# The first expert's first list closed with batch 3, its tokens turned inside attention's last iterations

## The chip, the cores and the metric

The kernel runs on one core of a Trainium2 chip. The metric is the time of one launch on the device in microseconds (us), as the median over runs; lower is better. The core has a matrix engine (PE, whose weight loads the profile shows as PEld), three engines for elementwise work (DVE, ACT, POOL) and a queue that only issues transfers (SP). Each engine works through its own instructions in order and waits on semaphores for the others. POOL also issues the indirect transfers, those whose rows are picked by a list of indices.

## The reference

Local and global attention, followed by a mixture of experts with a skip test. What matters here:

```
attention, for each of 8 batches and 8 heads, head_dim 64:
    512 local queries see the 32 global keys and local keys at distance <= 32
    32 global queries see all 544 keys
x = attention output as (8 * 544, 512) rows
do = x @ w_skip > 0                      # other rows leave unchanged
e  = argmax(x @ w_gate)                  # one of 8 experts
g  = softmax(x @ w_gate)[e]
out[do] = x + g * (relu(x @ w1[e]) @ w2[e])      # w1 512 x 1024, w2 1024 x 512
```

Rows belong to a batch; row r of batch b is row 544 b + r of the output. For the inputs that the reference draws, 1980 rows pass the skip test, and the experts get 395, 171, 153, 289, 173, 371, 253 and 175 of them. Expert 0 gets 243, 7, 31, 7, 15, 3, 84 and 5 from the eight batches in turn.

## The kernel before

**Attention** is a loop over u = 0 to 33 (`NU` = 32 pairs of heads, four pairs to a batch, and two iterations to drain). It is written out by hand as a software pipeline: in iteration u the scores and exponentials of pair u (`scores`, L344) run beside the scaling (POOL, `scale`, L396), the transposes (`turn`, L432) and the values (`values`, `values_g`, L470 and L495) of pairs u-1 and u-2. `turn(0)` is copied out of PSUM by DVE, `turn(1)` by ACT. `gather_g` (L511) reduces the global queries' part on DVE. The order of the instructions on PE, DVE, ACT and POOL is the order of the program text (`manual_schedule`).

**Rows and routing.** When the four pairs of a batch are done, `batch_rows` (L651) turns its output into rows, writes them to `out` through SP (L543, L551) and computes the logits. Batches 5 and 6 have theirs in iterations 25 to 29; those of batch 7 begin in iteration 31 and end behind the loop (L814, L815). `route` (L574) makes a list of some twenty small steps for two batches together, (0,1), (2,3), (4,5), or for one, 6 and 7. The steps wait in `stages`; each call of `seam()`, seven in an iteration, takes one or two of them through `tick`. The running count of each expert stands in `base`, from which each token gets its slot in the expert's list `lst` in DRAM. The last stage puts the batch's sends into the queue `sends`: one indirect transfer from POOL (L639) for every 128 rows, which writes row number and gate weight to the slots. `send_some(n)` issues n of them.

**The first list.** The first 256 slots (`GRP`) of an expert are its first group. After batch 6 the count of expert 0 is lifted to at least 256 (L700), so no row of batch 7 lands in its first group. At the end of iteration 31 all stages are worked off, all sends issued and the group's list is read by SP (`slots`, L106); in iteration 32 DVE turns the row numbers to integers (`index`, L102) and POOL gathers the 256 rows into `xfirst` (`gather`, L119), two transfers of 128 rows out of the first seven batches' part of `out`.

**The experts.** Behind the loop the attention pools are released and `turn_x` (L832) makes the transposed input of the first group: for each of two halves four transposes on PE, a cast to float32r on ACT (`xh`) and the rest on DVE (`xl`). `ffn` (L848) then does 8 steps of 12 matmuls (`ph`), each followed by relu on ACT (`hh`) and its rest on DVE (`hlw`), and for each half 8 steps of 3 matmuls (`py`); `hook(i)` inserts other work after step i. In the first expert: after step 1 the steps of batch 7's routing, its sends and the reading of all other lists; after steps 4 to 7 the split of the second expert's weights; after step 9 `rest`, with the index and gather of the second expert's first group; after step 22 its `turn_x`. Weights arrive as float32 tiles `raw` through SP and are split in two parts by ACT and DVE (L181, L184). A group beyond the first is done behind it, at full width if more than 128 rows remain, otherwise by `ffn_half`.

## Time and profile before

| what | before |
|---|---|
| median of three runs | 502.44 us (500.73 to 504.15) |
| the profiled execution | 503.73 us |
| its span, first to last instruction | 502.0 us |
| mean granted clock of PE | 0.986 |
| PE busy | 455.9 us, 91% |
| DVE, ACT, POOL busy | 298.7, 289.6, 228.2 us |
| moved by DMA | 93.32 MB, mean 186 GB/s |

A row of the timeline has the start in us from the span's start, the length, engine, line, operation, output and inputs, shapes and count; in brackets stands the idle time of that engine just before and what ended it. A row of a group has busy time and the mean ns of one behind the bar. A row of the windows has for each engine its busy us with the number of instructions, then the granted clock of PE, the busy share of the DMA engines and GB/s. Matmuls are pipelined, so their lengths overlap; the distance from start to start is their pace.

### The profile page before, as it was taken

Reading aid. Unit: us, or ns where it says so; the run is one execution under the profiler, and the core shown is the slowest. Engines: PE = TensorE matmul, PEld = TensorE weight load, DVE = VectorE, ACT = ScalarE, POOL = GpSimd, SP = SyncE. Lnnn points to the kernel's source line nnn. Section 1 sums busy time; section 2 is a strip of 40 time slices with the busy share of each in tenths; the row PEclk is TensorE's granted clock in tenths of the full one; section 3 lists DMA queues with packets and bytes.
Section 4 is the critical chain, followed back from the end, with each engine's and each line's share of the span. In section 5 each row is a group of like instructions: output and inputs, shape, how many; then the busy total and the mean of one; then the engine's idle time right before and its main releaser. Section 6 shows DMA issues by size and latency. Waiting matters only on the chain. (4 is left out here: it accounts for less than half of the span.)

```text
span 502.0 us, 13663 instructions
## 1 busy us (share of the span) xinstructions
PE 455.9 (91%) x4962; PEld 368.5 (73%) x4962; DVE 298.7 (59%) x1221; ACT 289.6 (58%) x883; POOL 228.2 (45%) x236
## 2 busy tenths in 40 slices
PE   8799999999989998887698999999989999899991
PEld 3576767776666767666696979898968888688881
DVE  6886767877757767784453229684714757047310
ACT  4689999899868887764341208563514545145210
POOL 6656666669864677776246014323202341013300
PEclk9999999999999999999899999999999999899996
DMA  8899898889957788610547308883820949113100
GB/s 252 267 329 262 268 288 279 254 281 219 289 171 244 226 189 255 169 45 2 172 146 216 109 26 268 313 295 121 286 99 10 343 142 327 38 23 131 46 15 17
DMA packets 50545, 93.32 MB, mean 186 GB/s; under 512 B 15596, under 2 KB 19948, under 8 KB 50448
## 3 DMA queue, kind: packets, MB, share of 16 engines
q1 hardware_dynamic: 44624, 81.83, 52.0%
q0 software_dynamic: 5824, 10.25, 6.2%
q8 instruction: 55, 0.90, 0.9%
q14 instruction: 42, 0.34, 0.3%
HBM read 82.91 MB, written 14.67 MB: 194 GB/s over the span
## 5 line engine op out<-in xcount | busy, mean ns | idle before, releaser
L368 ACT ACTIVATE prob<-prob,nmx 128x160 f32<-128x160 f32 x256 | 106.4, 418 | 17.9 <-DVE nmx L363 15.7
L398 POOL TENSOR_TENSOR prob<-prob,inv 128x640 f32<-128x640 f32 x64 | 80.3, 1257 | 61.1 <-DVE ing L428 24.0
L863 ACT ACTIVATE hh<-ph 128x256 fp32r<-128x256 f32 x72 | 27.7, 385 | 83.2 <-PE ph L858 71.8
L940 POOL DMA_INDIRECT out_dram<-yo,six x12 | 12.2, 1018 | 134.6 <-DVE yo L939 116.7
L874 PE MATMUL py<-w2h,hh 128*128 128x512 f32 x144 | 57.2, 397 | 0.0
L874 PE MATMUL py<-w2h,hlw 128*128 128x512 f32 x144 | 56.9, 395 | 0.0
L874 PE MATMUL py<-w2l,hh 128*128 128x512 f32 x144 | 56.7, 394 | 0.0
L351 PE MATMUL pss<-ks,qs 64*64 64x160 f32 x1024 | 51.5, 305 | 3.1 <-DVE nmx L363 1.6
L864 DVE SCALAR_TENSOR_TENSOR hlw<-ph,hh 128x256 fp32r<-128x256 f32 x72 | 30.3, 421 | 32.4 <-ACT hh L863 29.6
L351 PEld LDWEIGHTS pss<-ks,qs 64*64 64x64 f32 x1024 | 34.1, 134 | 20.9 <-issue 15.2
L858 PE MATMUL ph<-xh,w1h 128*128 128x256 f32 x288 | 46.4, 283 | 3.2 <-ACT xh L844 1.5
L482 PEld LDWEIGHTS pv<-ptT,vw 128*64 128x64 f32 x1024 | 39.4, 137 | 13.3 <-issue 3.9
L368 ACT ACTIVATION_READ_ACCUMULATOR prob<-prob,nmx 128x1 f32 x256 | 48.4, 189 | 0.0
L482 PE MATMUL pv<-ptT,vw 128*64 128x64 f32 (+1 forms) x1024 | 44.2, 237 | 3.4 <-ACT ptT L441 1.6
L858 PE MATMUL ph<-xh,w1l 128*128 128x256 f32 x288 | 45.5, 280 | 0.0
L858 PE MATMUL ph<-xl,w1h 128*128 128x256 f32 x288 | 45.4, 280 | 0.0
L858 PEld LDWEIGHTS ph<-xh,w1h 128*128 128x128 f32 x288 | 39.3, 191 | 5.9 <-issue 3.8
L639 POOL DMA_INDIRECT lst<-dat,slu x34 | 34.3, 1008 | 18.0 <-DVE cni L959 9.6
L858 PEld LDWEIGHTS ph<-xh,w1l 128*128 128x128 f32 x288 | 39.1, 190 | 0.0
L858 PEld LDWEIGHTS ph<-xl,w1h 128*128 128x128 f32 x288 | 39.0, 190 | 0.0
L438 PE MATMUL pst<-ident,prob 128*128 128x128 f32 x256 | 36.6, 281 | 2.5 <-POOL prob L398 1.2
L184 DVE TENSOR_TENSOR w1l<-raw,w1h 128x1024 fp32r<-128x1024 f32 x28 | 34.1, 1220 | 6.6 <-ACT w1h L181 4.1
(178 smaller groups left out, 942.3 us busy)
## 6 DMA issues: line engine op xcount, KB each, us to landing
raw<-in_w_dram SPq DMA_DIRECT2D x60, 512.0 KB
vw<-in_v_dram SPq DMA_DIRECT2D x32, 512.0 KB
ks<-in_kT_dram SPq DMA_DIRECT2D x32, 400.0 KB
out_dram<-xr SPq DMA_DIRECT2D x32, 256.0 KB
qs<-in_qT_dram SPq DMA_DIRECT2D x31, 256.0 KB
vgs<-in_vgl_dram SPq DMA_DIRECT2D x32, 64.0 KB
raw<-in_w_dram POOLq DMA_DIRECT2D x4, 512.0 KB
lst<-dat,slu POOLq DMA_INDIRECT x34
```

What stands on the lines that cost most here:

```text
L184: eng.tensor_sub(lo, raw, hi.bitcast(F32))
L351: nc.tensor.matmul(banks[odd][head(h ^ odd), j * W:(j + 1) * W], q[head(h), w * QB:(w + 1) * QB], window(k[head(h)], w), start=True, stop= ...
L368: nc.scalar.activation(pt[:, i, :], pt[:, i, :], AF.Exp, bias=nmx[:, i:i + 1], scale=-1.0, accum_out=sums[:, i, 0:1],)
L398: nc.gpsimd.tensor_mul(pt[:, sl, :], pt[:, sl, :], inv[:, sl].unsqueeze(2).to_broadcast([P, 4, W]),)
L438: nc.tensor.transpose(pst[:, i * P:(i + 1) * P], pt[:, 4 * hf + i, 0:KW], ident)
L482: nc.tensor.matmul(pv[head(h), j * 96:j * 96 + n], vv[:, w, head(h)], ptT[:, w, h ^ odd, 0:n], start=j == 0, stop=False, skip_group_check= ...
L639: ins = nc.gpsimd.indirect_dma_start(out=lst, out_offset=bass.IndirectOffsetOnAxis(ap=slu[:, t:t + 1], axis=0), in_=dat[:, bs[j], t - 4 * ...
L858: nc.tensor.matmul(ph[:, 0:GRP], hl[a][:, c, f * P:(f + 1) * P], bb[:, c, :], start=i == 0, stop=i == 3 * NC - 1,)
L863: nc.scalar.activation(hh[:, f, :], ph[:, 0:GRP], AF.Relu)
L864: nc.vector.scalar_tensor_tensor(hlw[:, f, :], ph[:, 0:GRP], 0.0, hh[:, f, :].bitcast(F32), ALU.max, ALU.subtract,)
L874: nc.tensor.matmul(py, a[:, f, ts_], hl[bb][:, f, :], start=f == 0 and i == 0, stop=f == NF - 1 and i == 2,)
L940: ins = nc.gpsimd.indirect_dma_start(out=out, out_offset=bass.IndirectOffsetOnAxis(ap=sidx, axis=0), in_=yo, in_offset=None, bounds_check= ...
```

## The change

The list of expert 0 is closed after the routing of batches 2 and 3 instead of after batch 6. It is read in iteration 29, its index and gather stand in iteration 30, and the gather reads only the first four batches' part of `out`. `turn_x` and the tiles of the first `xh` and `xl` move ahead of the loop, into the pool that lives throughout; iterations 32 and 33 turn one half of the tokens each, with the cast in two parts. The sends that are ready in iterations 29 to 31 are issued later: two in iteration 29, none in 30, two in 31, the others at the seams of iterations 32 and 33 (before: four at the end of 29, one at each seam of 30 and 31 and four at their ends, and all that were left at the end of 31). The memsets of `xsecond` and `xmore` move from the start of the experts into `rest`, ahead of the gathers there.

```diff
+    xs = [
+        [const.tile([P, NC, GRP], F32R, name=f"x{part}{i}") for part in "hl"] for i in range(1)
+    ]
+
+    def turn_x(xg, i, ts=range(NSUB)):
+        xh, xl = xs[i]
+        for t in ts:
+            pt = ps_t("xt")
+            for c in range(NC):
+                nc.tensor.transpose(
+                    pt[:, c * P:(c + 1) * P], xg[:, t, c * P:(c + 1) * P], ident
+                )
+            p3 = pt.rearrange("p (c n) -> p c n", n=P)
+            ts_ = slice(t * P, (t + 1) * P)
+            step = NC if len(ts) > 1 else NC // 2
+            for c in range(0, NC, step):
+                nc.scalar.copy(xh[:, c:c + step, ts_], p3[:, c:c + step])
+            nc.vector.tensor_sub(xl[:, :, ts_], p3, xh[:, :, ts_].bitcast(F32))
+        return xh, xl
...
-                if b == B - 2:
+                if b == B // 2 - 1:
                     stages.append(
                         lambda: nc.vector.tensor_scalar_max(base[:, 0:1], base[:, 0:1], float(GRP))
                     )
...
                 def seam():
                     tick(1 if u < NU - 4 else 2)
-                    if u >= NU - 2:
+                    if u >= NU:
                         send_some(1)
...
                     cur.scores(1)
+                if u == NU - 3:
+                    slots(first, 0)
+                if u == NU - 2:
+                    index(first, 0)
+                    gather(xfirst, six[:, 0, 0, :], B // 2 * S)
+                if u >= NU:
+                    turn_x(xfirst, 0, (u - NU,))
                 while subs:
                     subs.pop()()
...
-                if u == NU:
-                    index(first, 0)
-                    gather(xfirst, six[:, 0, 0, :], (B - 1) * S)
...
-                send_some(2 if u < NU - 3 else 4)
+                send_some(4 if u >= NU else 2 if u != NU - 2 else 0)
                 seam()
                 prev, old = cur, prev
                 if u == NU - 1:
                     tick(len(stages))
-                    send_some(len(sends))
-                    slots(first, 0)
...
-    for t in (xsecond, xmore):
-        nc.gpsimd.memset(t, 0.0)
...
+    xs.append([f1.tile([P, NC, GRP], F32R, name=f"x{part}1") for part in "hl"])
...
-        x2 = turn_x(xfirst, 0)
+        x2 = xs[0]
         tick(13)
...
         def rest():
+            for t in (xsecond, xmore):
+                nc.gpsimd.memset(t, 0.0)
             index(slice(1, E), 0)
             index(slice(0, E), 1)
             gather(xsecond, six[:, 1, 0, :])
```

## What was expected

> **What bounds the kernel now.** I read the page's head first, then the timeline of TensorE (PE) around the end of attention, then the granted clock in short windows, then the queues of DVE, ACT, POOL and SP at that place.
>
> ```profile
> span 502.0 us, 13663 instructions
> PE 455.9 (91%) x4962; PEld 368.5 (73%) x4962; DVE 298.7 (59%) x1221; ACT 289.6 (58%) x883; POOL 228.2 (45%) x236
> ```
>
> PE is busy 91% of the span, so the time falls only where PE's idle or slow stretches fall. The timeline of PE has one such stretch where the first expert begins (start, length, line, count, idle before it and what ended it):
>
> ```profile
> 239.95 0.63 PE L531 MATMUL pr<-idw,xTg 128*128 128x137 f32 x4
> 241.66 0.63 PE L837 MATMUL xt<-ident,xfirst 128*128 128x128 f32 x4 [1.08 <-DMA xfirst<-out_dram,six]
> 244.42 0.63 PE L837 MATMUL xt<-ident,xfirst 128*128 128x128 f32 x4 [2.13 <-DMA xfirst<-out_dram,six]
> 245.73 1.22 PE L858 MATMUL ph<-xh,w1h 128*128 128x256 f32 x4 [0.68 <-ACT xh L844]
> 250.24 0.72 PE L858 MATMUL ph<-xh,w1h 128*128 128x256 f32 x4
> 253.15 0.63 PE L858 MATMUL ph<-xh,w1h 128*128 128x256 f32 x4
> 254.56 0.63 PE L858 MATMUL ph<-xh,w1h 128*128 128x256 f32 x4
> 269.06 0.40 PE L874 MATMUL py<-w2h,hlw 128*128 128x512 f32 x1
> 270.81 1.29 PE L837 MATMUL xt<-ident,xsecond 128*128 128x128 f32 x8 [1.35 <-DMA xsecond<-out_dram,six]
> ```
>
> Attention's last matmul ends at 240.58 and the expert's first starts at 245.73: 5.15 us, of which 3.89 are idle (1.08, 2.13, 0.68) and 1.26 turn the tokens. What ends the waits is the gather of xfirst. A second wait, 1.35 us before 270.81, is for the gather of xsecond. Then the clock (window, PE busy, ..., PEclk, DMA share, GB/s):
>
> ```profile
> 241.90:245.30 3.40, 1.02 (x8) 0.57 (x6) 0.69 (x1) 0.80 (x2) 0.64 (x1) 1.00 0.79 275
> 245.30:248.70 3.40, 2.97 (x14) 2.97 (x15) 2.73 (x13) 0.62 (x3) 0.00 (x0) 0.50 0.34 79
> 269.20:272.60 3.40, 2.02 (x13) 1.30 (x11) 0.51 (x1) 1.05 (x2) 3.10 (x5) 1.00 0.70 229
> 429.60:433.00 3.40, 1.80 (x9) 1.28 (x9) 0.68 (x1) 0.65 (x2) 0.00 (x0) 1.00 0.03 10
> 433.00:436.50 3.50, 3.50 (x10) 2.69 (x10) 0.01 (x1) 0.00 (x0) 0.00 (x0) 0.51 0.02 5
> ```
>
> After a window with PE busy 1.02 us of 3.4 the clock is 0.50 for the next 3.4; 1.80 us busy lets it fall too, 2.02 us does not. So the gap costs twice: the expert's groups of 12 matmuls come every 1.41 us later on (253.15 to 254.56), but the first two take 245.73 to 250.24 = 4.51, where 2 x 1.41 and some 0.28 for the counts between them make 3.10. Loss: 1.41 us.
>
> **The change part by part.** *The turn leaves the seam.* Gather, eight transposes, casts and subtractions are no longer between 240.58 and 245.73: -5.15 us, and with the gap the slow clock behind it: -1.41 us.
>
> *It comes back in iterations 32 and 33,* half the tokens in each, ahead of work that these end on:
>
> ```profile
> 233.55 0.65 ACT L509 COPY xT<-pv 128x256 f32<-128x256 f32 x2 [2.27 <-PE pv L501]
> 233.95 0.29 DVE L516 TENSOR_REDUCE xTg<-pv 128x32 f32<-128x128 f32 x1 [2.40 <-ACT xT L509]
> 233.64 1.10 PE L438 MATMUL pst<-ident,prob 128*128 128x128 f32 x8
> 234.68 0.65 DVE L441 COPY ptT<-pst 128x512 f32<-128x512 f32 x1
> 235.43 0.80 PE L482 MATMUL pv<-ptT,vw 128*64 128x96 f32 x14 [0.69 <-ACT ptT L441]
> 237.50 0.65 ACT L509 COPY xT<-pv 128x256 f32<-128x256 f32 x2 [2.13 <-PE pv L501]
> 238.74 1.78 ACT L536 COPY xr<-pr 128x256 f32<-128x256 f32 x4 [0.59 <-PE pr L531]
> L845 DVE TENSOR_TENSOR xl<-xt,xh 128x512 fp32r<-128x512 f32 x20 | 13.1, 687 | 25.4 <-ACT xh L844 25.4
> L844 ACT CAST xh<-xt 128x256 fp32r<-128x256 f32 x4 | 1.3, 375 | 11.7 <-PE xt L837 11.7
> ```
>
> In iteration 32 PE turns after the values at 233.6 (0.63, beside idle time). ACT casts twice (375 ns each, a half per cast) after its two xT copies, until about 234.85. DVE's subtraction (687 ns) waits for that and stands ahead of the reduction at 233.95 and the ptT copy at 234.68: the reduction starts near 235.5 instead of 233.95, so ptT and the values of the last pair come 1.55 us later, at 236.98. In iteration 33 the second half stands between the values and the last rows: the casts push ACT's copies of the rows back, one row bank waits for the subtraction. I followed each from 236.98: the values take 2.07 (235.43 to 237.50) to 239.05; xT copies and casts, which overlap as the two in 0.65 do, take ACT to 240.3; the subtraction ends at 241.0; the third of the five rows goes then, the fifth when the second's copies have left their bank at 241.9, and its 0.63 on PE ends at 242.6. So the first expert starts at 242.7 where the rows ended at 240.58: 2.1 us. Bounds: 1.26, the PE time of the turn alone, if DVE and ACT hide theirs, to 3.45 (two casts and a subtraction, 1.44, and PE's 0.63, twice, less the 0.69 idle at 235.43). I stay between, since the queues' order puts the subtraction ahead but PE's own part into idle time.
>
> *The clock in the tail.* From the end of the pst transposes (233.64 and 1.10, moved by PE's half microsecond, 235.25) to 236.98 PE would idle 1.73 us, so a 3.4 us window that holds all of it has about 1.7 busy: below 1.80. Where the windows lie decides, about evenly. Price: nothing to 1.41 us; I take 0.6, nearer the middle since PE waits for ACT and DVE there anyway. That transposes count as busy is read from the window at 269.20: 1.29 of its 2.02 busy us are transposes, and the clock stayed at 1.00. The Trainium skill, "TensorE: Matmul & The Clock Gate", Part 4, says that transposes do not count as PE-busy the same way; by that, 233.6 to 236.98 would be one idle stretch and the drop near certain, which is the second rival below.
>
> *List and gather, earlier.* The list is read in iteration 29, the gather issued in 30:
>
> ```profile
> 203.21 1.06 POOL L639 DMA_INDIRECT lst<-dat,slu  x1 [0.48 <-issue]
> 218.73 0.32 DVE L363 CUSTOM_DVE_ANT_0 prob<-pss,m_last 128x160 f32<-128x160 f32 x1
> 221.70 1.01 POOL L639 DMA_INDIRECT lst<-dat,slu  x1 [0.17 <-issue]
> 231.77 0.98 POOL L639 DMA_INDIRECT lst<-dat,slu  x1 [0.30 <-DVE pgT L466]
> 235.80 0.34 SPq L106 DMA_DIRECT2D lt<-lst  x1
> 237.86 1.08 POOL L119 DMA_INDIRECT xfirst<-out_dram,six  x1 [3.82 <-DVE six L102]
> ```
>
> SP waits for the last send of batches 0 to 3, issued at 203.21. Before, list and index followed their last send (231.77) in 4.03 and 6.09 us; here that gives 207.2 and 209.3. Behind the list on SP stand the rows of batch 6, behind DVE's index the rest of iteration 30. The index stands after the last score of 218.73, ten us later: 0.17 us on DVE, no wait. POOL's two gathers (1.1 us each) take the place of two sends at 221.70, with the same scaling behind them: nothing. PE wants the tokens only at 233.6.
>
> *Sends, memsets, base.* Of the twelve sends of batches 4 to 6, two stay in iteration 29, two come at the end of 31 and eight in 32, behind the last scaling, 1.3 us apart: POOL is busy until about 243 instead of 233. Cover: it has nothing due until batch 7's sends (below). The two memsets (0.95 each) move behind those, into a wait of 7.18. The closing of the list is one small DVE instruction moved to an earlier batch. Routing the reference's inputs gives expert 0 288 of its 395 tokens in the first four batches, so the list of 256 is full and no group of tokens is added or lost.
>
> *What is late next.* Batch 7's list and the second expert's weights:
>
> ```profile
> 246.31 0.47 DVE L688 TENSOR_REDUCE lg<-lgb 128x45 f32<-128x180 f32 x1
> 252.14 1.03 POOL L639 DMA_INDIRECT lst<-dat,slu  x1 [9.60 <-DVE cni L959]
> 257.33 1.27 POOL L639 DMA_INDIRECT lst<-dat,slu  x1 [0.30 <-issue]
> 265.78 1.05 POOL L119 DMA_INDIRECT xsecond<-out_dram,six  x1 [7.18 <-issue]
> SPq L543 <- DMA xfirst<-out_dram,six: 3.2, 1, 3.2
> 248.79 1.79 SPq L165 DMA_DIRECT2D raw<-in_w_dram  x4
> 255.44 1.05 ACT L181 CAST w1h<-raw 128x1024 fp32r<-128x1024 f32 x1 [0.29 <-DMA raw<-in_w_dram]
> L184 DVE TENSOR_TENSOR w1l<-raw,w1h 128x1024 fp32r<-128x1024 f32 x28 | 34.1, 1220 | 6.6 <-ACT w1h L181 4.1
> L864 DVE SCALAR_TENSOR_TENSOR hlw<-ph,hh 128x256 fp32r<-128x256 f32 x72 | 30.3, 421 | 32.4 <-ACT hh L863 29.6
> ```
>
> The chain 246.31, 252.14, 257.33, 265.78, 270.81 starts when the last rows' logits are out: 243.2 instead of 246.31, and its counts on PE come after two fast groups, 245.6 instead of 249.97 by the group starts. So sends and gather move up 4.4 to 5 us with PE, and the wait of 1.35 stays or shrinks by that lead of up to half a microsecond: I take -0.3 (from 0 to -1.35). On SP the last rows wait 3.2 us for the gather of xfirst (both touch batches 4 to 6); the new gather reads only the first four batches, so that wait goes, and the weights, issued when those rows have landed, go at about 246.3 instead of 248.79. PE is 4.4 earlier, they only 2.5: ACT's cast waits about 2 us more, but what stands behind it (the last three of eight steps' hh and hlw) is used only from the sixth step of the second layer on. That layer starts at 242.7 + 8 x 1.41 + 0.28 = 254.3 and makes a step in 0.70 (15 of them from 250.24 + 6 x 1.41 = 258.70 to 269.46), so the sixth step asks for hlw at 258.2; a cast at 253 has it ready by 255.7. Nothing.
>
> Sum: -5.15 - 1.41 + 2.1 + 0.6 - 0.3 = **-4.2 us**. The profiled execution took 503.73 (502.0 its span, 1.7 around it), which gives 499.5; it lies 1.29 above the median 502.44, and from that the same difference gives **498.2**.
>
> **The rivals.** *Weights late.* If SP's weights come no earlier than now, the cast stays at 255.44; the sixth hlw then waits for the cast (1.05), its subtraction on DVE (1.22) and its own 0.42, to 258.13, and the next two follow 1.64 apart: 259.77 and 261.41. Against PE's demand at 258.2, 258.9 and 259.6 the last is 1.8 late: gain 2.4, 500.0. For it: 248.79 follows many waits; against it: the row with 3.2.
>
> *The clock falls in the tail.* If the transposes there do not count, the matmul-free stretch is 3.35 us (233.6 to 236.98), a whole window, and the values and rows behind it pay 1.41 instead of 0.6: gain 3.4, 499.0. For it: 1.80 busy us were too few at 429.60; against it: the window at 269.20, by which the trace does not agree with the page.
>
> *Everything hidden.* The tail keeps its clock and batch 7's list gains on PE, so that the 1.35 goes: 5.15 + 1.41 - 2.1 + 1.35 = 5.8, 496.6. For it: POOL idles 9.60 before 252.14.
>
> *The list decides.* If POOL's eight late sends, or their landing, hold back batch 7's, PE runs ahead and waits for xsecond at 270.81 as now: gain 0, 502.4. It needs POOL to be 4 us later than 243.
>
> *Slower.* The list read in iteration 29 lands late, and DVE's index and POOL's gather stop iteration 30. Place: after 218.73. Each us behind about 219 costs one; from 223.4 on the change loses, and at 228.5 it is 5 us slower, 507.5. Against it: ten us of slack at the pace of 231.77 to 235.80.
>
> **How the numbers follow.** The forecast has 0.45, everything hidden 0.24, the clock 0.10, weights late 0.11, the list 0.06, slower 0.04. A measurement here tells about 1%, 5.0 us, from no change. Faster by over that: the hidden case mostly, and a quarter of the forecast: 0.35. Slower 0.04, the rest 0.61. The range goes from 495.6 (hidden, 496.6, with a us for the runs' spread of 500.73 to 504.15) to 501.3 (weights late, 500.0, with the tail at its bound of 3.45 instead of 2.1). Outside lie the list, the slower case and the edges of the others.
>
> **What would show it.** PE's gap before the first L858 goes from 5.15 to under 0.5, with xt<-xfirst at about 233.6 and 239; the first group takes 1.4 us; DVE's ptT copy of iteration 32 comes 1.5 us later after its values; POOL's sends end near 243; SP's rows wait for no gather; the wait before xt<-xsecond is 1.35 or less. It is wrong if PE waits in iterations 30 to 31, if the first group still runs at half clock, or if the wait before xsecond grows by what the seam gained.

## The result, and the profile after

The changed kernel took 505.48 us (median of 15 runs, 503.00 to 509.56) against 501.79 (15 runs, 499.72 to 505.17) for the kernel before beside it: ratio 1.0073, 95% interval 1.0044 to 1.0103. It is 0.4 to 1.0% slower, where 498.2 and a gain of 4.2 us had been forecast; the time lies outside the range of 495.6 to 501.3.

Its line numbers are up to 20 higher than those of the kernel before (L529 is the xT copy of L509, L203 the turn, L859 the `ph` matmul, L864 its relu). The head of its page, and PE's timeline around the end of attention and at the turn of the second expert's tokens:

```profile
span 506.4 us, 13664 instructions
PE 458.7 (91%) x4962; PEld 373.8 (74%) x4962; DVE 297.9 (59%) x1221; ACT 290.4 (57%) x885; POOL 228.6 (45%) x236
```

```profile
232.76 0.65 PE L203 MATMUL xt<-ident,xfirst 128*128 128x128 f32 x4
...
236.32 2.20 PE L502 MATMUL pv<-ptT,vw 128*64 128x96 f32 x32 [2.04 <-issue]
...
239.88 0.48 PE L521 MATMUL pv<-pgT,vgs 64*64 64x128 f32 x3 [0.16 <-issue]
...
245.04 1.74 PE L551 MATMUL pr<-idw,xT 128*128 128x137 f32 x6 [1.92 <-ACT xT L529]
246.42 1.22 PE L859 MATMUL ph<-xh,w1h 128*128 128x256 f32 x4
...
253.56 0.72 PE L859 MATMUL ph<-xh,w1h 128*128 128x256 f32 x4
...
273.93 0.63 PE L203 MATMUL xt<-ident,xsecond 128*128 128x128 f32 x4 [1.01 <-DMA xsecond<-out_dram,six]
275.58 0.66 PE L203 MATMUL xt<-ident,xsecond 128*128 128x128 f32 x4 [1.02 <-DMA xsecond<-out_dram,six]
...
278.54 0.74 PE L859 MATMUL ph<-xh,w1h 128*128 128x256 f32 x4 [0.73 <-ACT xh L210]
```

Up to 236.32 all goes as forecast: the tokens are there, the first half is turned at 232.76, the last pair's values start 0.7 us earlier than the 236.98 worked out. Then the tail is lost. The last values end at 240.36 and the rows, which need ACT's copies of them, go on only at 245.04. The first expert's third group starts at 253.56 (250.24 before), and behind xsecond the next group at 278.54 (274.65 before). ACT in the same stretch, the copy of ptT and the next instruction on its queue:

```profile
234.86 0.59 ACT L461 COPY ptT<-pst 128x512 f32<-128x512 f32 x1 [0.58 <-PE pst L458]
244.34 0.65 ACT L529 COPY xT<-pv 128x256 f32<-128x256 f32 x2 [8.89 <-PE pr L551]
```

The copy at 244.34 waits only for the last values. They end at 240.36, so PE's signal reaches ACT 3.98 us late. (The bracket names a later matmul: four signals of PE, due between 239.73 and 243.12, are recorded together, from 244.32 to 244.48.) Before, the same copy (237.50) started 0.03 us behind them. POOL and SP meanwhile:

```profile
232.78 1.01 POOL L659 DMA_INDIRECT lst<-dat,slu  x1 [0.16 <-issue]
...
241.74 0.97 POOL L659 DMA_INDIRECT lst<-dat,slu  x1 [0.30 <-issue]
255.63 0.97 POOL L659 DMA_INDIRECT lst<-dat,slu  x1 [12.92 <-DVE cni L960]
...
268.59 1.05 POOL L119 DMA_INDIRECT xsecond<-out_dram,six  x1 [4.75 <-issue]
```

```profile
246.30 6.48 SPq L563 DMA_DIRECT2D out_dram<-xr  x8
254.16 1.79 SPq L165 DMA_DIRECT2D raw<-in_w_dram  x4
265.51 0.38 SPq L106 DMA_DIRECT2D lt<-lst  x1
```

Eight sends, back to back, fill 232.78 to 242.71; the late signal falls into them. The second expert's weights (raw) go at 254.16 instead of 248.79, the lists are read at 265.51 instead of 261.69. And the clock, by windows of PE's work (columns as before):

```profile
236.60:240.00 3.40, 3.24 (x50) 2.78 (x46) 0.00 (x0) 0.00 (x0) 2.75 (x3) 0.50 0.02 1
240.00:243.40 3.40, 1.62 (x9) 0.95 (x9) 0.00 (x0) 0.00 (x0) 2.10 (x3) 1.00 0.02 1
243.40:246.80 3.40, 1.76 (x8) 1.76 (x9) 1.16 (x4) 1.57 (x5) 0.00 (x0) 0.50 0.09 7
246.80:250.20 3.40, 3.40 (x17) 3.40 (x17) 0.35 (x2) 1.02 (x3) 0.00 (x0) 0.50 0.47 172
```

Three windows at half clock where the kernel before had one. So there were two candidates from the start, the sends and the clock, and the runs below brought a third and a fourth:

- **Theory 1:** a run of sends, back to back on POOL, delays PE's signals to ACT and DVE.
- **Theory 2:** the gap that the turn opens ahead of the last values halves the clock, and that alone makes the loss.
- **Theory 3:** the list decides by itself: batch 7's sends land only when the second expert's first weights have landed, so xsecond comes a fixed time behind these, whatever PE gained.
- **Theory 4:** the late sends lie on the DMA engines while batch 7's rows are written; the rows land late, and the weights, whose buffers wait for rows and sends, with them.

### The profile page after: what moved, and what is told of

Same layout as the page of the kernel before. It is cut to its first block, busy times and chain, and to the rows that moved or that the text cites. A ratio compares the mean times of both kernels' runs of the same rounds, so it can differ in the third digit from the quotient of the medians.

```text
span 506.4 us, 13664 instructions
## 1 busy us (share of the span) xinstructions
PE 458.7 (91%) x4962; PEld 373.8 (74%) x4962; DVE 297.9 (59%) x1221; ACT 290.4 (57%) x885; POOL 228.6 (45%) x236
## 5 line engine op out<-in xcount | busy, mean ns | idle before, releaser
L864 ACT ACTIVATE hh<-ph 128x256 fp32r<-128x256 f32 x72 | 27.6, 385 | 82.8 <-PE ph L859 66.6
L859 PE MATMUL ph<-xh,w1h 128*128 128x256 f32 x288 | 47.1, 287 | 4.2 <-PEq L1013 2.0
L502 PEld LDWEIGHTS pv<-ptT,vw 128*64 128x64 f32 x1024 | 40.7, 141 | 13.8 <-issue 4.8
L502 PE MATMUL pv<-ptT,vw 128*64 128x64 f32 (+1 forms) x1024 | 45.5, 243 | 4.1 <-issue 2.7
L859 PE MATMUL ph<-xh,w1l 128*128 128x256 f32 x288 | 47.0, 285 | 0.0
L859 PE MATMUL ph<-xl,w1h 128*128 128x256 f32 x288 | 46.2, 283 | 0.0
L859 PEld LDWEIGHTS ph<-xh,w1h 128*128 128x128 f32 x288 | 40.0, 194 | 6.6 <-issue 5.5
L859 PEld LDWEIGHTS ph<-xh,w1l 128*128 128x128 f32 x288 | 40.0, 193 | 0.0
L859 PEld LDWEIGHTS ph<-xl,w1h 128*128 128x128 f32 x288 | 39.8, 194 | 0.0
```

The lines of the kernel that those rows point to most:

```text
L502: nc.tensor.matmul(pv[head(h), j * 96:j * 96 + n], vv[:, w, head(h)], ptT[:, w, h ^ odd, 0:n], start=j == 0, stop=False, skip_group_check= ...
L859: nc.tensor.matmul(ph[:, 0:GRP], hl[a][:, c, f * P:(f + 1) * P], bb[:, c, :], start=i == 0, stop=i == 3 * NC - 1,)
L864: nc.scalar.activation(hh[:, f, :], ph[:, 0:GRP], AF.Relu)
```

## The experiments

The table gives for each run the ratio to the kernel before beside it (95% interval), the start of the values of pair 28 in iteration 30, and, counted from there, the start of the third `ph` group, of the first load of raw, of the reading of the lists, and of the next `ph` group behind the turn of xsecond. All starts are from the timelines. Lag: ACT's last xT copies start over 3 us behind the last values. Without the late sends (G2, K2, M2) the tokens in them reach no expert, so these times are no gain that a kernel could keep.

| kernel | ratio | it. 30 | third ph | raw | lists | next ph | lag |
|---|---|---|---|---|---|---|---|
| before (first profile) | 1 | 213.41 | 36.83 | 35.38 | 48.28 | 61.24 | no |
| before, with blocks in later experts (E4) | | 209.93 | 37.47 | 35.58 | 49.56 | 62.02 | no |
| changed | 1.0073 (1.0044 to 1.0103) | 214.95 | 38.61 | 39.21 | 50.56 | 63.59 | yes |
| changed, second (F1) | 1.0001 (0.9967 to 1.0035) | 210.58 | 30.03 | 36.14 | 46.76 | 61.81 | no |
| changed, third (H1) | 1.0053 (1.0029 to 1.0076) | 212.31 | 38.69 | 39.28 | 49.46 | 63.07 | yes |
| changed, fourth (K1) | 1.0021 (0.9987 to 1.0054) | 209.84 | 30.01 | 35.87 | 46.98 | 61.04 | no |
| changed, fifth (M1) | 1.0035 (0.9993 to 1.0076) | 213.31 | 38.81 | 39.37 | 50.15 | 65.10 | yes |
| sends as before (E1) | 1.0033 (1.0006 to 1.0060) | 210.25 | 35.96 | 36.57 | 49.43 | 63.00 | no |
| turn behind the loop (E2) | 0.9996 (0.9968 to 1.0024) | 210.71 | 29.77 | 34.99 | 46.08 | 59.36 | no |
| the same (K3) | 1.0009 (0.9969 to 1.0049) | 210.56 | 29.77 | 34.59 | 45.18 | 58.52 | no |
| sends behind the rows (E3) | 1.0084 (1.0055 to 1.0112) | 212.45 | 31.58 | 37.86 | 50.31 | 62.75 | no |
| changed, raw behind the lists (F2) | 0.9977 (0.9944 to 1.0010) | 213.55 | 30.03 | 44.69 | 42.21 | 58.64 | no |
| turn behind the loop, raw behind the lists (F3) | 0.9968 (0.9936 to 1.0001) | 210.57 | 31.33 | 45.83 | 43.35 | 60.34 | no |
| before, raw behind the lists (F4) | 1.0073 (1.0040 to 1.0106) | 211.04 | 37.86 | 52.01 | 49.84 | 66.02 | no |
| without the late sends (G2, one run) | | 210.12 | 30.02 | 30.93 | 43.19 | 56.00 | no |
| the same (K2, one run) | | 209.77 | 30.02 | 31.26 | 43.27 | 55.59 | no |
| the same (M2) | 0.9900 (0.9856 to 0.9944) | 212.88 | 31.61 | 32.35 | 44.99 | 58.89 | no |
| half of the late sends earlier (G3) | 0.9965 (0.9937 to 0.9992) | 209.59 | 31.59 | 34.34 | 47.48 | 59.95 | no |
| gather in the tail (G1) | 0.9904 (0.9870 to 0.9938) | 212.58 | 32.17 | 32.84 | 45.52 | 59.64 | no |
| the same (K4) | 0.9911 (0.9873 to 0.9949) | 209.93 | 31.73 | 32.24 | 44.47 | 58.49 | no |

### Sends as before (E1)

```diff
-                    if u >= NU:
+                    if u >= NU - 2:
                         send_some(1)
...
-                send_some(4 if u >= NU else 2 if u != NU - 2 else 0)
+                send_some(2 if u < NU - 3 else 4)
...
                     tick(len(stages))
+                    send_some(len(sends))
```

> The changed kernel with the sends of batches 4 to 6 issued as in the kernel before (four at the end of iteration 29, the rest at the seams and ends of 30 and 31, none in 32 or 33). Theory 1 (a run of sends, back to back on POOL, delays PE's signals to ACT and DVE): the xT copies of the last pair start within 0.7 us of the end of its values (4 us in the changed kernel), the rows follow as in the kernel before, the xr copies end near 243 us, the first ph group starts near 243, and the time is 497 to 499 against the 501.8 before. Theory 2 (the gap that the turn opens ahead of the last values halves the clock, and the halved clock alone makes the loss): the values of the last pair still take about 4 us, the clock still falls twice between 236 and 250, and the time is 504 to 506.

The ratio is 1.0033, 499.40 against 497.72 us. By time neither theory is met; the timeline shows why. ACT's and PE's rows in the tail, and one wait of PE in iteration 31:

```profile
238.41 0.65 ACT L529 COPY xT<-pv 128x256 f32<-128x256 f32 x2 [3.69 <-PE pv L521]
```

```profile
225.33 1.28 PE L551 MATMUL pr<-idw,xT 128*128 128x137 f32 x4 [2.88 <-DVE lgb L560]
...
237.31 1.08 PE L521 MATMUL pv<-pgT,vgs 64*64 64x128 f32 x16
```

The last values run at half clock (1.08 where full clock takes 0.67), and still the copy starts 0.02 us behind their end at 238.39: so here half clock by itself makes no lag. (F1 below has no lag with the sends either, on the same chip number, so this run alone does not part the theories.) From iteration 32 to the third group this kernel takes 15.61 us (230.60 to 246.21), before 19.31: that is the gain. But with sends and two gathers in front of it on POOL the scaling of iteration 31 starts at 223.60, DVE and the rows behind it wait, and iteration 31 takes 14.18 us (216.42 to 230.60) instead of 10.16; behind PE's waits there the clock is 0.50 from 223.77 to 230.59, which is a part of the loss. POOL has no room there for both. The early gather is what pushed the sends into the tail.

### Turn behind the loop (E2)

```diff
-                if u >= NU:
-                    turn_x(xfirst, 0, (u - NU,))
...
-        x2 = xs[0]
+        x2 = turn_x(xfirst, 0)
```

> The changed kernel with the turn of the first tokens left behind the loop, as in the kernel before; the early list and gather and the late sends stay. Theory 1: nothing is turned in iterations 32 and 33, but the eight sends stand there, so ACT's xT copies still start 2 to 4 us behind the last values, the last rows end 3 us or more later than 240.6, and the time is 502 to 506. Theory 2: the tail runs as in the kernel before, the rows end at 240.6, the turn follows at once without the waits of 1.08 and 2.13 for the gather, and the time is 498 to 500.

No lag, in spite of eight sends in the tail, and the third group 7 us earlier than before; and still 0.9996. So theory 1 as it stood, for any chip, fell here. Theory 2's 498 to 500, a gain beside 501.8, did not come either: the gain was made and lost again. ACT, by what it waited for from 240 to 256:

```profile
ACT w1h L181 <- DMA raw<-in_w_dram: 7.3, 1, 7.3
```

The weights had not landed when ACT came to their cast, and the last relus stand behind that cast on ACT's queue.

### Sends held back until the rows are done (E3)

```diff
-                    if u >= NU:
-                        send_some(1)
...
-                send_some(4 if u >= NU else 2 if u != NU - 2 else 0)
+                send_some(0 if u >= NU else 2 if u != NU - 2 else 0)
...
                 batch_rows(B - 1, k, (1,))
+            nc.gpsimd.tensor_copy(gatep, lgb[B - 1][:, 4, 3, :])
+            send_some(len(sends))
```

> The changed kernel, with the ten sends that are left after iteration 31 held back until the last row's logits are out: one small copy on POOL reads them ahead of the sends. Theory 1: iterations 32 and 33 run free, xT copies within 0.7 us of the values, the first ph group at about 243; the delay moves to the first ph groups, whose relu then waits 1 to 4 us in places behind its group, and batch 7's sends start near 255; 499 to 504. Theory 2: the tail is that of the changed kernel, values of about 4 us and half clock, and the time is 504 to 508, since batch 7's sends come later as well.

1.0084, as a ratio inside theory 2's band (504 to 508 of 501.8), by time (502.27) inside theory 1's; but the tail is free and at full clock, as theory 1 had it, and nothing lags. The sends held back are eight, with batch 7's five behind them, not the ten of the expectation. What is late is raw, and SP's waits from 236 to 262 name the cause:

```profile
SPq L166 <- DMA lst<-dat,slu: 6.3, 2, 3.7
```

The buffers of raw lie where attention's tiles were, and the slots (`slu2`) of batches 4 and 5 are among these: raw waits until their sends have landed. A send that is moved back moves the weights back.

### Sends, plain transfers and POOL work in later experts (E4)

```diff
             hook(f)
+            if f == 2 and bank is ps_v and e in (2, 4, 6):
+                nc.gpsimd.tensor_copy(gatep, hlw[:, f, 0:8].bitcast(F32))
+                for i in range(32 if e == 6 else 8):
+                    if e == 2:
+                        again[0](i % 5, spare[i // 5])
+                    elif e == 4:
+                        nc.gpsimd.dma_start(spare[2][i * P:(i + 1) * P, :], dat[:, B - 1, i % 5, :])
+                    else:
+                        nc.gpsimd.memset(xmeas, 0.0)
```

> The kernel before, with three blocks added on POOL, each released by the third hlw of an expert's first layer: in expert 2 eight indirect writes of batch 7's slots into spare memory, back to back; in expert 4 eight plain transfers of 128 x 8 bytes from POOL into spare memory; in expert 6 32 memsets of 128 x 256, some 8 us of POOL work without any transfer. Theory 1: in expert 2 the relu of steps 4 to 8 starts up to 1 to 4 us behind the end of its ph group on PE (0.1 to 0.3 elsewhere), in expert 6 it does not; expert 4 tells whether it is the indirect form or any run of transfers from POOL. Theory 2: the relu follows its group by 0.1 to 0.3 us in all three. Time: 502 to 506, as the relu has three PSUM banks of slack.

No relu is late in any of the three, but only the first block tests it: in expert 2 three relus follow its start (327.93), each 0.04 us behind its group, while in experts 4 and 6 the transfers (397.50) and the memsets (459.43) begin with the layer's last relu (397.63 and 459.57). The single run took 507.49 against 497.72; PE's waits from 300 on are 6.7 us at three branches behind the groups (4.5 the longest), which no theory had, and whose cause was not followed. With F1 below, on the same chip number and also without lag, this says only that sends do not always delay PE's signals. It also served as a profile of the kernel before on such a chip, up to expert 2.

### The weights behind the lists (F2, F3, F4)

The same edit on the changed kernel, on the one with the turn behind the loop, and on the kernel before:

```diff
-                for _ in range(8 if e else 4):
+                for _ in range(8 if e else 0):
                     weights[e + 1].load()
...
             slots(slice(0, E), 1)
+            for _ in range(4):
+                weights[1].load()
...
-                todo = {i: split for i in (4, 5, 6, 7)}
+                todo = {i: split for i in (18, 19)}
+                todo[23] = lambda: (split(), split())
```

> The changed kernel with the second expert's first four weight loads on SP moved behind the reading of the lists, and their splits from steps 4 to 7 to steps 18, 19 and 23. Theory 3: the sends of batch 7 land within 3 us of their issue, the list is read some 3 to 6 us earlier than in the changed kernel as it is, PE does not wait for xsecond, and the time falls by 2 to 5 us, to 0.995 to 1.002 of the kernel before. Theory 1: what is lost is lost in iterations 32 and 33, and the move gains at most the wait of 1 to 2 us for xsecond: 1.002 to 1.006.

> Early list and gather and late sends, the turn left at the seam (as in the run with the turn behind the loop), and the weight loads and splits moved as in the run before this one. In the run without that move the third ph group started some 7 us earlier in relation to the attention before it than in the kernel before, and 5 of these were lost to relus behind late weights and the end of the wait. Theory 3: they stay: xsecond is there before PE asks, no relu waits, 0.986 to 0.991 of the kernel before (5 to 7 us). Theory 1: 0.997 to 1.000, the wait for the weights only changes its place.

> The kernel before with the same move of the weight loads and splits alone: the control. Theory 3: the list is read earlier, the wait of 1.35 us ahead of xsecond goes, nothing else: 0.995 to 0.999. If the move by itself brings as much as the run with the turn at the seam, then that run's gain is not the change's.

Theory 3 is right in its first half: in all seventeen profiles with the weights ahead of the lists, these are read 10.2 to 14.0 us behind the first raw, lag or not. Without the weights in flight the lists are read 5.0 us behind the start of batch 7's last send in all three (250.74 to 255.76 in F2), with them 9.6 in F1 (247.79 to 257.34). Its second half is not borne out as it stood: nothing of 5 to 7 us comes back against the kernel before (0.9977, 0.9968), and the control is slower, 1.0073. But against that control, which has the same move, F2 and F3 are 3.3 and 4.4 us faster (498.65 and 497.57 against 501.98): with the weights out of the way a part of the gain stays, and the move itself, 3.1 us in the kernel before, eats it. PE's waits in F2, from 240 to 275:

```profile
PE xt L203 <- DMA xsecond<-out_dram,six: 3.5, 1, 3.5
```

The two megabytes of raw now travel beside the gather of xsecond, which takes longer: from its first issue to the second transfer's landing 8.4 us in F2 (259.12 to 267.50), 5.1 in F1 (264.22 to 269.29). Moving the weights only changes which transfer they hold up.

### The changed kernel again (F1, H1)

> The changed kernel as it is, beside the next three on one chip, with a second profile. Theory 1 (a run of sends delays PE's signals): ACT's xT copies of the last pair again start 2 to 4 us behind the end of the last values, and the first ph group is the stretch that costs. Theory 3 (the list decides: batch 7's sends land only when the second expert's first weights, issued on SP behind the last rows, have landed, so xsecond comes a fixed time after those weights are issued, whatever PE gained): with or without that delay the list is read 11 to 13 us after the first raw load is issued. Time for both: 1.003 to 1.010 of the kernel before.

> The changed kernel a third time. Open is whether the xT copies of the last pair starting 4 us behind their values, seen in its first profile and not in its second, belong to the change. Theory 1: they come back, with 1.004 to 1.010 of the kernel before. Theory 4: ACT copies within 0.7 us of the values, raw goes out 4 us or more behind the last row's issue, the relus of the first layer wait some 5 us for the casts, and the ratio is 0.997 to 1.004.

The second profile has no lag, and there the change makes no difference, 1.0001. The third has it again, 3.96 us, at 1.0053. Theory 4 was formed from the second. PE and ACT there, in the tail and at the first cast of the weights:

```profile
231.76 1.34 PE L502 MATMUL pv<-ptT,vw 128*64 128x96 f32 x32 [1.85 <-issue]
...
235.24 0.72 PE L859 MATMUL ph<-xh,w1h 128*128 128x256 f32 x4
```

```profile
233.82 0.65 ACT L529 COPY xT<-pv 128x256 f32<-128x256 f32 x2 [3.29 <-PE pv L521]
...
253.34 1.04 ACT L181 CAST w1h<-raw 128x1024 fp32r<-128x1024 f32 x1 [7.76 <-DMA raw<-in_w_dram]
```

The tail is better than forecast: full clock, the first `ph` group starts 8.83 us behind the values of iteration 32 (226.41), before 14.80, and runs between the last rows. SP, and PE's waits from 240 to 275:

```profile
235.46 5.89 SPq L563 DMA_DIRECT2D out_dram<-xr  x8
246.72 1.79 SPq L165 DMA_DIRECT2D raw<-in_w_dram  x4
257.34 0.38 SPq L106 DMA_DIRECT2D lt<-lst  x1
```

```profile
PE py L875 <- ACT hh L864: 4.1, 3, 1.8
PE py L875 <- DVE hlw L865: 1.2, 2, 0.6
```

SP has issued the last row at 241.35, but raw goes at 246.72, 5.4 us later (1.4 before: 247.41 to 248.79): the rows land up to 246.64, with eight sends on the same engines, the last of them landing at 244.60. Against attention, raw is not earlier at all (36.14 and 35.38 in the table). PE waits 5.3 us for relus and their rests behind the casts, and the lists are read late as well. Behind these waits the clock is 0.50 from 257.98 to 264.81 (in K1 from 257.06 to 263.89), a second price of them. Some 7 us of gain by the third group, none at the next `ph`.

### Without the late sends (G2)

```diff
                 if u == NU - 1:
                     tick(len(stages))
+                    sends.clear()
```

> The changed kernel without the eight sends of iterations 32 and 33: the tokens in them get no entry in their experts' lists, so later gathers and scatters move fewer rows, while PE's work stays the same. Theory 4: batch 7's rows land within 1.5 us of their issue, the first raw load goes out 1.5 us behind the last row (5.4 in the second profile of the changed kernel), the relus of the first layer wait for no cast or under 1.5 us in all (5.3 there), the list is read 5 to 6.5 us behind batch 7's last send (9.5 there). Theory 3: the list and xsecond come as late as there, and PE waits 4 us or more ahead of xsecond.

```profile
235.00 4.68 SPq L563 DMA_DIRECT2D out_dram<-xr  x8
241.05 1.79 SPq L165 DMA_DIRECT2D raw<-in_w_dram  x4
253.31 0.38 SPq L106 DMA_DIRECT2D lt<-lst  x1
```

SP's rows of this kernel: raw 1.4 us behind the last row, lists 5.9 us behind the start of the last send (247.37), no PE wait for a relu. The clock stays at 1.00 there. The next `ph` comes 5.8 us earlier than in F1 (56.00 and 61.81; another chip, also without lag). That is theory 4, with a share of theory 3 left: PE still waits 3.0 us for xsecond. The later gathers move fewer rows here, so the 5.8 is a little too large.

### Half of the late sends earlier (G3)

```diff
-                send_some(4 if u >= NU else 2 if u != NU - 2 else 0)
+                send_some({NU - 3: 4, NU - 2: 1, NU - 1: 3}.get(u, 2 if u < NU else 4))
```

> The changed kernel with four of the eight late sends issued earlier, where POOL idles: four sends at the end of iteration 29 instead of two, one at the end of 30, three at the end of 31, and four instead of eight in 32. Theory 4: these four have landed before the last rows are written, so raw goes out about 1.5 us behind the last row and the relus wait under 2 us; the tail itself runs as in the changed kernel, so 0.988 to 0.994 of the kernel before. Theory 3: 0.998 to 1.003, the gain goes at xsecond.

0.9965 (0.9937 to 0.9992): a small gain, 497.61 against 499.92, between theory 4's band (up to 0.994) and theory 3's (from 0.998). Raw goes 1.4 us behind the last row (242.55 to 243.93), as expected; the relus cost PE 3.0 us (1.9 and 1.1), where under 2 were expected; perhaps raw now meets batch 7's sends, which was not tested.

### List early, gather in the tail (G1)

The kernel before with four edits: the list of expert 0 closed, read and indexed as in the changed kernel, the gather in iteration 32 and out of the first four batches' rows, sends and turn as they were.

```diff
-                if b == B - 2:
+                if b == B // 2 - 1:
...
+                if u == NU - 3:
+                    slots(first, 0)
+                if u == NU - 2:
+                    index(first, 0)
                 while subs:
...
                 if u == NU:
-                    index(first, 0)
-                    gather(xfirst, six[:, 0, 0, :], (B - 1) * S)
+                    gather(xfirst, six[:, 0, 0, :], B // 2 * S)
...
                     send_some(len(sends))
-                    slots(first, 0)
```

> The kernel before with the list of expert 0 closed after batch 3, read in iteration 29 and turned to integers in iteration 30, as in the changed kernel, but the sends as before (none in 32 or 33), the gather in iteration 32 behind the last scaling, and the turn behind the loop. Theory 4 (the late sends lie on the DMA engines while batch 7's rows are written, the rows land late, and the second expert's weights, whose buffers wait for these landings, with them; PE's gain is then given back at relus behind the weights' casts and at xsecond): here nothing of that kind runs late, the tokens are there when the rows end, the first ph group starts about 3 us earlier than before and at full clock, the first raw load goes out 2 to 3 us earlier, and 3 to 4.5 us stay to the end: 0.991 to 0.995 of the kernel before. Theory 3 (the list decides by itself): PE waits 3 us longer for xsecond, 0.998 to 1.001.

0.9904 (0.9870 to 0.9938), 495.23 against 499.92, at the good end of what theory 4 had, and faster than the kernel before by 4.7 us. PE at the seam, and SP:

```profile
239.77 1.04 PE L839 MATMUL xt<-ident,xfirst 128*128 128x128 f32 x8
241.58 0.74 PE L860 MATMUL ph<-xh,w1h 128*128 128x256 f32 x4 [0.77 <-ACT xh L846]
```

```profile
238.49 4.85 SPq L543 DMA_DIRECT2D out_dram<-xr  x8
245.42 1.79 SPq L165 DMA_DIRECT2D raw<-in_w_dram  x4
258.10 0.38 SPq L106 DMA_DIRECT2D lt<-lst  x1
```

The turn follows the rows without a wait for the gather, the groups start at full clock, and raw and lists come 2.5 and 2.8 us earlier than before (table: 32.84 and 45.52 against 35.38 and 48.28). The turn needs no place inside attention; what the seam needed was an early list and a gather that waits for nothing.

### On a chip with the lag and on one without

What was open: whether the lag needs the sends. First on a chip that showed none (K1 to K4):

> The changed kernel beside the next three on one chip. Two of its three profiles show ACT's last xT copies 4 us behind their values, and there the kernel before took 501.5 to 501.8; one does not, and there it took 498.9. If the lag is there again, the kernel before should take over 501 here and the ratio be 1.004 to 1.010; if not, under 500 and 0.997 to 1.003.

> The changed kernel without the eight sends of iterations 32 and 33, whose tokens get no entry in their lists. Where the run before this one shows the lag of 4 us, theory 1 (the run of sends delays PE's signals) has none here: xT copies within 0.7 us of the values, the third ph group 29 to 31 us behind the values of iteration 30 instead of some 38.6. If the halved clock ahead of the last values made the lag, it is here as well.

> Early list and gather and late sends with the turn behind the loop. Where the first run of this call shows the lag of 4 us, theory 1 has one of 2 to 4 us here too, at the xT copies or the rows, since the sends stand there; if it takes the halved clock of the turn's gap as well, there is none and the third ph group starts 30 us behind the values of iteration 30.

> List and index early, sends as before, gather in iteration 32, turn behind the loop. With the lag or without it in the first run of this call, no send stands in 32 or 33, so 0.988 to 0.994 of the kernel before.

The kernel before took 498.49 there, nothing lagged, and the runs repeat F1, G2, E2 and G1 (table). G1 and K4 are the only runs of that kernel, so what it brings on a chip with the lag is not shown. Then on one that showed it; the kernel before took 501.81, and the ratio of M1, 1.0035, is just under the 1.004 that was expected:

> The changed kernel once more, to find a chip on which its last xT copies lag: then the kernel before takes over 501 beside it and this one 1.004 to 1.010 of that; else under 500 and 0.997 to 1.003.

> The changed kernel without the eight sends of iterations 32 and 33, on the same chip. If the run before this one shows the lag: by theory 1 none here, xT copies within 0.7 us of the values; if the halved clock made it, the same 4 us here.

ACT's copies of the last pair in these two, with the late sends and without:

```profile
242.69 0.65 ACT L529 COPY xT<-pv 128x256 f32<-128x256 f32 x2 [8.85 <-remote]
```

```profile
237.70 0.65 ACT L529 COPY xT<-pv 128x256 f32<-128x256 f32 x2 [3.29 <-PE pv L521]
```

With them the copy starts 3.7 us behind the last values (238.24 + 0.70 = 238.94), without them 0.03 (237.00 + 0.67 = 237.67). ("Remote" is a source that the profile doesn't tell.) On one chip, with one difference, the lag goes with the sends. The halved clock goes too in M2, so these rows alone don't part the two. What parts them is a second lag, at batch 7's sends, which the first profile of the kernel before has too. ACT there:

```profile
248.69 0.38 ACT L863 ACTIVATE hh<-ph 128x256 fp32r<-128x256 f32 x1 [1.18 <-PE ph L858]
...
255.44 1.05 ACT L181 CAST w1h<-raw 128x1024 fp32r<-128x1024 f32 x1 [0.29 <-DMA raw<-in_w_dram]
259.38 0.39 ACT L863 ACTIVATE hh<-ph 128x256 fp32r<-128x256 f32 x1 [2.89 <-PE ph L858]
```

The group of this relu starts at 254.56 and the next one at 255.98, and ACT is free from 256.49; it starts at 259.38, 2.89 us late, at full clock, during five sends (252.14 to 258.60). PE had free banks then and lost nothing. The relu at 248.69, with no sends about, starts 0.04 us behind a group that ran at half clock (0.50 from 245.28 to 248.69). The same sixth relu in M1 and in M2, whose batch 7 sends stay:

```profile
261.31 0.38 ACT L864 ACTIVATE hh<-ph 128x256 fp32r<-128x256 f32 x1 [2.87 <-PE ph L859]
```

```profile
252.24 0.39 ACT L865 ACTIVATE hh<-ph 128x256 fp32r<-128x256 f32 x1 [1.44 <-PE ph L860]
```

It is late at full clock in all five profiles with a lag anywhere: 2.89 us before, 2.15 in the first of the changed kernel, 2.86 in H1, 2.87 in M1, 1.44 in M2; in the other profiles it starts within 0.05 us, in E4, G1 and K4 with their sends in the same place. So the lag goes with sends and needs no half clock, and theory 1 holds where these five ran. What marks that place is open: H1 lagged on a chip numbered 11, and so were the chips of E1 to F4, which did not.

## Why the prediction was wrong

**The step that failed** is the one on the sends: "Of the twelve sends of batches 4 to 6, two stay in iteration 29, two come at the end of 31 and eight in 32", with the cover "it has nothing due until batch 7's sends", costed at nothing. The cover was true of POOL, which is done at 242.71 as written ("busy until about 243"), and false of what the sends do elsewhere. Their price:

- With the lag, M1 against M2: 7.2 us at the third group (38.81 and 31.61), 6.2 at the next `ph`, 6.6 by medians (504.12 and 497.56).
- Without it, F1 against G2: nothing at the third group, 5.2 at raw, 5.8 at the next `ph`. K1 against K2: 4.6 and 5.5.

So either way about 6 us go where nothing had been set, and the forecast of -4.2 becomes +2; measured were +3.69 first, +2.6 and +2.3 in the other runs with the lag (the interval of the last includes no change), and none that can be told in the two without, where the tail gained more than was forecast. The rest of the sum came out near: without the sends the next `ph` comes 5.2 us sooner than before in G2 (56.00 and 61.24), 5.7 in K2 and 2.4 in M2, a little too much since their later gathers move fewer rows.

**The turn leaves the seam, -5.15 and -1.41:** right without the lag; with it the first groups ran at half clock again (0.50 from 243.41 to 250.24 in the first profile). **It comes back, +2.1 and +0.6:** too much. Without the lag, from iteration 32's values to the third group, 14.20 us (226.41 to 240.61) stand against 19.31 before, -5.1 where the terms make -3.86. The last pair's values came 5.35 us behind those of iteration 32 instead of 4.50, 0.85 for the 1.55 given, and the first `ph` matmuls ran between the last rows. The half clock, given even odds, came in the three profiles with the lag (gap ahead of the values 2.02 to 2.04 us) and in E1, and not in F1 and K1, with E1's gap of 1.85 us. The line that the forecast drew, a drop below 1.80 us of work in 3.4, does not hold (last section).

The Trainium skill, "TensorE: Matmul & The Clock Gate", Part 4, says that transposes do not count as PE-busy in the same way; by that the stretch from the turn to those values would have been idle and a drop near certain. In F1 the values behind it took 1.34 us, full clock, but there that stretch lies across two of the clock's steps of 3.41 us. A step in F2, 208.48 to 211.89, tells more: 2.66 us of transposes and no other matmul, and the clock stayed at 1.00 behind it (last section). So the trace does not agree; the row that the forecast had weighed against it held.

**List and gather, earlier:** right; in no profile of the changed kernel did index or gather stop iterations 30 and 31, and the rival that made it slower by that way was not what happened.

**Weights "at about 246.3":** the wait for the gather went, as written. That raw also waits for the sends of batches 4 and 5 and for rows behind them on the DMA engines was not seen. **"Weights late"**, a rival of 0.11, is what happened without the lag, by a different cause and at 5.3 us of PE's waits instead of 1.8. **"The list decides"**, 0.06, asked for POOL to be late; the list was late with POOL in time, since its sends land late beside the weights. Its time, no change, is what F1 and K1 took, but its condition was not met.

**The wait ahead of xsecond, -0.3:** from 1.35 to 2.03 in the first profile. Of what would make it wrong by the text, the first group at half clock came, in the profiles with the lag; a growth of this wait by what the seam gained did not.

## What to carry to other kernels

A transfer that is moved into a quiet place of its issuing engine is not free there: ask what else is on the DMA engines in that stretch, whose buffers are held until it has landed, and who waits for signals meanwhile. A gain at a seam counts only as far as the next thing that is fed by transfers; follow each of them (rows, weights, list, gather) to its issue and landing, and count its time from a fixed point in attention, not from where PE stands. When a transfer can be issued early enough for its user only by pushing others late, issue it later and let its user wait less: the early list with the gather in the tail brought 1% on two chips without the lag, the early gather nothing.

## What the runs showed of the hardware

- Runs of small indirect writes (128 x 8 bytes, 1.28 us apart) delay PE's signals to ACT in some places, by 1.4 to 2.9 us during five and 3.7 to 4.0 during eight, and in others not at all: five profiles of the changed kernel, three with 3.7 to 4.0 us, two with under 0.1. The kernel before took 501.5 to 501.8 beside the three and 497.7 to 499.9 beside all runs without. What differs there stays open (the chip's number does not tell), and so does why the signal is late.
- Small writes land late when they are issued just behind large ones: from the start of the last send to the list it is 4.9 to 5.0 us without the weights in flight (F2 to F4); with them, 8.4 to 9.8 where that send starts 1.1 to 4.4 us behind the first raw (F1, K1, E2, K3, G3), and 3.6 to 6.3 where it starts 6.0 us or more behind. The Trainium skill, "DMA: Bandwidth & Descriptors", Queues, rings and completion order, says that a DMA engine's increment of the semaphore lands only after that engine's earlier writes, across its queues. The rows that landed 5.3 us after the last issue with the sends about, where raw followed by 1.4 without, agree with that.
- The clock changes at steps of 3.41 us (in E1 at 223.77, 230.59, 237.42 and 240.84). Three such steps:

```profile
234.01:237.42 3.41, 1.56 (x41) 1.46 (x44) 1.80 (x5) 0.58 (x1) 0.00 (x0) 1.00 0.00 0
```

```profile
232.37:235.78 3.41, 1.56 (x34) 1.35 (x34) 1.87 (x5) 0.90 (x3) 2.50 (x4) 1.00 0.03 3
208.48:211.89 3.41, 2.66 (x22) 2.03 (x21) 0.86 (x5) 3.03 (x9) 2.53 (x3) 1.00 0.76 232
```

The first, from E1, is followed by 0.50; the other two, from F2, by 1.00. So 1.56 us of work came out both ways, as it did not drop the clock in E3, G3 and M2 either, and the busy share alone does not foretell the drop. The last of the three is transposes only, and they kept the clock up. In F1 no step around the gap had under 2.33 us of work, so its full clock says nothing of the share.
